# Moving the splits of three segment weights and the loads of an x chunk in a gated attention mix, and giving two value tiles other PSUM banks

## The chip, the cores and the metric

The kernel runs on one core of a Trainium2 chip. The metric is the device time of one execution in microseconds; the median of the runs is compared.

## What is computed

A gate mixes two attention layers over the same input `x` of 2048 rows by 512, with 32 heads of 16:

```python
q, k, v = (x @ wqkv) ...                      # A: full softmax attention
p = _softmax(q @ k.T * Dh ** -0.5)
a = (p @ v) @ wo
...
for s in range(4):                            # B: segments of 512 rows
    a_dot = softmax(qs @ ks.T * scale + mask) @ vs
    a_mem = (phi(qs) @ M) / (phi(qs) @ z + 1e-6)
    outs.append(g * a_mem + (1.0 - g) * a_dot)
    M = M + phi(ks).T @ vs;  z = z + phi(ks).sum(over rows)
b = outs @ wo_B
...
g = _sigmoid((x * gate_w).sum(-1))
out = g * a + (1 - g) * b
```

All is float32. `phi(t)` is `t + 1` where t is positive and `exp(t)` elsewhere. B has its own weights `b_wq`, `b_wk`, `b_wv`.

## The kernel before, in words

**Halves.** Each fp32 operand of a projection is split into a high half (a cast to fp32r on ACT, `copy`) and a low half (the difference, on DVE or POOL, `tensor_sub`). A product is three matmuls (line 360: low-high, high-low, high-high). The names end in `h` and `l`: `wvh` and `wvl` are the halves of a `v` weight, `xbh` and `xbl` those of a tile of tag `xb`.

**Slots.** The projections come first, ahead of the attention loop. PE's program is cut into slots of twelve matmuls of 128x128 by 128x512 (`slot`, line 362; all of them bear line 366), each slot into four places (0 to 3) of three matmuls. What other engines do is hung on a slot and a place: `post_at(n, place, f)` names the slot by number, `post(slots, place, f)` counts from the current one. This sets only the order of the instructions in each engine's program; when an instruction runs is decided by its waits. The slots that matter here:

| slots | what PE computes |
|---|---|
| 0 to 7 | A's `v` of x chunks 0 and 1 (a chunk is 512 rows) |
| 8 to 15 | A's `q` tiles of chunks 0 and 1 |
| 16 to 22 | pair tiles of chunks 0 and 1: `k` and the rest of `q` |
| 23 to 26 | v2: A's `v` of the third chunk, one slot for each 128 rows |
| 27 to 30 | v3: A's `v` of the fourth chunk |
| 31 to 37 | pair tiles of chunks 2 and 3: fourteen products m0 to m13, two in a slot |
| 38 to 41 | B's `q` of chunk 0 |
| 42 to 45 | B's `v` of chunk 0 |
| 46 to 49 | B's `k` of chunk 0 |
| 50 on | B's chunk 1, then 2 and 3, in the same order, with the memory's products and the first score maxima between |

**Banks.** PSUM is handed out by three pools: `pr` (two banks, "query products"), `me` (two) and `sm` (four). A pool hands out its buffers in the order in which they were released; a tile that gets a buffer waits until the readers of its former tile are done. ACT reads a `v` product (line 537, `vs<-pair` or `vs<-pr`) and a `q` or `k` product (line 432, `full`); the pair products are read by ACT (line 492, `p`) and DVE (lines 476, 500, 502: `full` and `u`). v3 has its banks from `me`, `me`, `pr`, `pr`; m2 and m3 follow it in the two `me` banks, in slot 32.

**The tile `vs`.** The four copies of a chunk's `v` fill one tile `vs`, which SP stores to DRAM (line 532, `vdA<-vs`). The tile has one buffer, so the copies of the next chunk wait until that store has landed, and so does a POOL memset of its last column (line 536 for v3).

**Staged loads.** `staged` (line 584) takes a weight or x chunk of 512x512 in two halves of two 128x512 loads each, at two given slots and places, into tiles of tag `raw` (three buffers for a half each) or `small` (tag `ph`, four buffers of 128x512), and splits its four pieces at four given slots and places (line 575 the cast on ACT, line 576 the difference). The B weights are loaded by POOL's queue (line 569). `halves` (line 380) does the same for the x chunks of B, with loads by SP's queue at slot `load_slot` and splits from `split_slot` on (lines 402 and 403); `betas` (line 751) is hung on slot 30 and begins with ACT's activation of `gh` at line 752, in front of which stands a table load.

**Other users of the engines there.** ACT makes the casts of the pair tiles' results (line 479) and of `q` and `k` (line 433), SP stores them, DVE and POOL make their low halves (line 485, line 440).

Of the kernel before, what the change touches and what calls it, by code (L numbers as in the profile page):

```python
# [24 lines left out]
KT = D // 128  # L25
# [22 lines left out]
def gated_mix(ctx, tc, x, xT, wqkv, a_wo, b_wq, b_wk, b_wv, b_wo, beta, gate_w, out):  # L48
    nc = tc.nc
# [283 lines left out]
    with ExitStack() as p0:  # L333
        wp = p0.enter_context(tc.tile_pool(name="wp", bufs=1))
        raws = p0.enter_context(tc.tile_pool(name="raws", bufs=3))
        xp = p0.enter_context(tc.tile_pool(name="xp", bufs=1))
        vp = p0.enter_context(tc.tile_pool(name="vp", bufs=1))
        wk = p0.enter_context(tc.tile_pool(name="wk", bufs=2))
# [15 lines left out]
        now = [0]  # L354
        posted = {}

        def post(slots, place, f):
            posted.setdefault((now[0] + slots, place), []).append(f)
# [17 lines left out]
        def post_at(n, place, f):  # L376
            posted.setdefault((n, place), []).append(f)


        def halves(pool, tag, src, load_slot, split_slot, tiles=None, queue=nc.sync, eng=nc.vector):  # L380

            hold = {}

            def load(i):
                t = tiles[i] and tiles[i]() if tiles else None
                if t is None:
                    t = raws.tile([128, 2, D], F32, tag="raw", name="raw")
                if isinstance(t, list):
                    for k in range(2):
                        queue.dma_start(t[k], src[256 * i + 128 * k:256 * i + 128 * k + 128])  # L390
                        hold["raw", 2 * i + k] = t[k]
                else:
                    queue.dma_start(t, src[256 * i:256 * i + 256].rearrange("(k p) d -> p k d", p=128))
                    for k in range(2):
                        hold["raw", 2 * i + k] = t[:, k]

            def split(k):
                if k == 0:
                    hold[0] = pool.tile([128, KT, D], F32R, tag=tag + "h", name=tag + "h")
                    hold[1] = pool.tile([128, KT, D], F32R, tag=tag + "l", name=tag + "l")  # L400
                w = hold["raw", k]
                nc.scalar.copy(hold[0][:, k], w)
                eng.tensor_sub(hold[1][:, k], w, hold[0][:, k].bitcast(F32))
            if load_slot is None:
                load(0)
                load(1)
            else:
                ls = load_slot if isinstance(load_slot, tuple) else (load_slot,) * 2
                post_at(ls[0], 2, lambda: load(0))
                post_at(ls[1], 3, lambda: load(1))  # L410
            for k in range(KT):
                post_at(split_slot + k // 2, 2 * (k % 2), lambda k=k: split(k))
            return hold

        def xchunk(c):
            return xT[:, c * CH:(c + 1) * CH]
# [107 lines left out]
        def v_tiles(side, w, xs, c, inner=True, behind_=0, banks_=None):  # L524
            vs = vp.tile([128, NG, 4, 4, 17], F32, tag="vs", name="vs")
            if not behind_:
                nc.gpsimd.memset(vs[:, :, :, :, 16:17], 1.0)

            def store():
                flat = vs.rearrange("p g b h e -> p g (b h e)")  # L530
                dst = vdA[:, :, c].rearrange("g p b e -> p g (b e)") if side == "A" else vdB[c].rearrange("p g b e -> p g (b e)")
                nc.sync.dma_start(dst, flat)

            def to_vs(b, ps):
                if b == 0 and behind_:
                    nc.gpsimd.memset(vs[:, :, :, :, 16:17], 1.0)
                nc.scalar.copy(vs[:, :, b, :, 0:16], ps.rearrange("p (g h e) -> p g h e", g=NG, h=4))
            banks = banks_ or [lambda: pr_ps.tile([128, D], F32, tag="pr", name="pr")] * 4
            if not inner:
                pss = [f() for f in banks]  # L540
                for k in range(KT):
                    slot([(pss[b], xs(p, k)[:, b * 128:(b + 1) * 128], w[q][:, k, :], k == 0 and n == 0, k == KT - 1 and n == 2)
                          for n, (q, p) in enumerate(((0, 0), (1, 0), (0, 1))) for b in range(4)])
                for b in range(4):
                    post(behind_, b // 2, lambda b=b: to_vs(b, pss[b]))
                post(behind_, 1, store)
                return vs
            for b in range(4):
                ps = banks[b]()
                whole(ps, lambda a, k: xs(a, k)[:, b * 128:(b + 1) * 128], lambda a, k: w[a][:, k, :])  # L550
                post(behind_, 0, lambda b=b, ps=ps: to_vs(b, ps))
                if b == 3:
                    post(behind_, 0, store)
            return vs
# [29 lines left out]
        def staged(t, src, raws_, splits, queue=nc.sync, keep=None, eng=nc.vector):  # L584

            kept = [] if keep is None else keep
            dest = []

            def load(i):
                kept.extend(raws_[i][0]())  # L590
                load_raw(src[256 * i:256 * i + 256], kept[2 * i:2 * i + 2], queue)

            def split(k):
                if not dest:
                    dest.extend(t())
                split_to(dest[0](k), dest[1](k), kept[k], eng)
            for i in range(2):
                post_at(raws_[i][1], raws_[i][2], lambda i=i: load(i))
            for k in range(KT):
                post_at(*splits[k], lambda k=k: split(k))  # L600
# [4 lines left out]
        def spread(n, place=0):  # L605
            return [(n + k // 2, place + 2 * (k % 2)) for k in range(KT)]
# [6 lines left out]
        xraw = {0: raw_tile(), 1: raw_tile()}  # L613
# [8 lines left out]
        wAv, wAq, wAk = weights("wv"), weights("wq"), weights("wk")  # L622
        xs = {0: in_pool("xa"), 1: in_pool("xb")}
# [27 lines left out]
        def s_split(i, x0, x1, eng=nc.vector):  # L651
            for k in range(2):
                src = (x1[2 + k], x0[k], x1[k], x0[2 + k])[i]
                split_to(ss[i][0][:, k], ss[i][1][:, k], src, eng)
# [65 lines left out]
        def tiles_w(key, tag):  # L720
            def f():
                xs["w"][key] = in_pool(tag) if tag == "xb" else weights(tag)
                return in_tile(xs["w"][key])
            return f
# [1 line left out]
        staged(tiles_x2, xchunk(2), ((raw_tile, 10, 0), (raw_tile, 10, 2)), spread(14), keep=xraw[2])  # L726
        staged(tiles_x3, xchunk(3), ((raw_tile, 11, 0), (small, 11, 2)), spread(17), keep=xraw[3], eng=P)
        staged(tiles_x0, xchunk(0), ((small, 15, 0), (small, 24, 2)), ((23, 1), (23, 3), (27, 1), (27, 3)))
        staged(tiles_w("q", "xb"), b_wq, ((raw_tile, 28, 0), (raw_tile, 28, 2)), spread(31, 1), nc.gpsimd)
        staged(tiles_w("v", "wv"), b_wv, ((raw_tile, 29, 0), (small, 29, 2)), spread(35, 1), nc.gpsimd)  # L730
        staged(tiles_w("k", "wk"), b_wk, ((raw_tile, 34, 0), (raw_tile, 34, 2)), spread(38, 1), nc.gpsimd)
        for k in range(2):
            post_at(18, 3, lambda k=k: s_sums(xraw[2], xraw[3], ((k, P),)))
        for n, i in enumerate((0, 2, 1, 3)):
            post_at((23, 24, 25, 26)[n], 3, lambda i=i: s_split(i, xraw[2], xraw[3]))
        gw = {}
        gmask = wk1.tile([128, NO, 2, DH], F32, name="gmask")
        for h in range(8):
# [33 lines left out]
        sm_bank = lambda: me_sm.tile([128, CH], F32, tag="sm", name="pair")  # L772
        pr_bank = lambda: pr_ps.tile([128, D], F32, tag="pr", name="pr")
# [5 lines left out]
                qk_tile(wAq, xs[c], o, qd["A", o, c], side="A")  # L779
        dk = {(o, c): kd["A", o, c] for o in range(NO) for c in range(NCH)}  # L780
        pair_tiles(wAk, tks, [flat(xs[0]), flat(xs[1])], ss, (0, 1), dk, V)
        v_tiles("A", wAv, lambda a, k: xs[2](a, k), 2, banks_=[sm_bank] * 4)
        v_tiles("A", wAv, lambda a, k: xs[3](a, k), 3, behind_=1, banks_=[me_bank, me_bank, pr_bank, pr_bank])
        pair_tiles(wAk, tks, [lambda a, k: xs[2](a, k), lambda a, k: xs[3](a, k)], ss, (2, 3), dk, P)

# [104 lines left out]
        for c in range(NCH):  # L890
            if c + 1 == NCH:
                load_gate(c)
                post(8, 2, gates)
            for o in range(NO):
                qk_tile(xs['w']['q'], xc, o, qd["B", o, c], pqs.append if c else None, bank=sm_bank if c == 0 and o > 1 else None)
            if c + 1 < NCH:
                xn = halves(*((xp, "xa") if c % 2 else (wp, "wq")), xchunk(c + 1), now[0], now[0] + (4 if c == 0 else 3))
            if c + 1 < NCH:
                post(2, 3, lambda c=c: load_gate(c))
            vs = v_tiles("B", xs["w"]["v"], flat(xc), c)  # L900
            for o in range(NO):
                then = (lambda pk, o=o, c=c, vs=vs: beside_max(lambda: mem_k(o, c, pk, vs))) if c + 1 < NCH else None
                qk_tile(xs['w']['k'], xc, o, kd["B", o, c], then)
            xc = xn
# [421 lines left out]
    n = 0  # L1326
# [81 lines left out]
```

## Time and profile before

| what | us |
|---|---|
| median of 3 runs (1750.44 to 1752.34) | 1751.22 |
| the profiled execution, its own time | 1751.74 |
| span of its trace | 1750.0 |
| PE busy | 1739.6 (99%) |
| DVE busy | 1597.9 (91%) |
| ACT busy | 1436.2 (82%) |
| POOL busy | 736.8 (42%) |
| mean granted TensorE clock | 1.000 of full speed |

The span is counted from the first instruction to the last; the execution's own time is 1.74 us longer. PE's busy time is summed from matmuls that overlap in the pipeline. All times of single instructions in the following are from the start of this span. A row of a timeline has the start, the duration, the engine, the line, the operation, the tiles (written from read) and the shapes; xN are N neighbours of one kind taken together, and brackets hold the idle time of the engine ahead of the row with what ended it.

### The profile page before, as it was taken

The page shows a single profiled execution, that of the slowest core. Times are in us where ns is not written, and L with a number is a line of the kernel's source. Part 1 is how long each engine was busy: PE and PEld are TensorE (multiplying, and loading weights), DVE is VectorE, ACT ScalarE, POOL GpSimd, SP SyncE. Part 2 cuts the span into 40 slices and gives each one's busy share as a digit, 9 for nine tenths or more (in the row PEclk, how much of TensorE's full clock was granted, in tenths as well). Part 3 has the DMA queues.
Part 4 walks back from the last instruction along what each step waited for, and adds up shares of the span by engine and source line. Part 5 has one row for each costly group of instructions (what it writes and reads, how often), then busy time and mean ns, then how long its engine had stood idle before and what let it go on. Part 6 is the DMA issues. An engine that isn't in the chain of part 4 may idle for free.

```text
span 1750.0 us, 41552 instructions
## 1 busy us (share of the span) xinstructions
PE 1739.6 (99%) x15205; PEld 886.2 (51%) x15205; DVE 1597.9 (91%) x3327; ACT 1436.2 (82%) x2763; POOL 736.8 (42%) x992
## 2 busy tenths in 40 slices
PE   9999999999999999999999999999999999999999
PEld 7877775444444444444444444444444444444445
DVE  7756778999999999999999999999999999999931
ACT  6544556888888888888898888888889889888884
POOL 3533232324262418353435353444344353535452
PEclk9999999999999999999999999999999999999999
DMA  6777667334453446454545454444444444544541
GB/s 210 246 241 249 214 214 215 112 107 138 116 157 96 136 135 191 130 143 124 149 127 143 130 143 136 133 136 130 148 125 150 119 132 126 152 115 146 147 156 63
DMA packets 149371, 261.62 MB, mean 149 GB/s; under 512 B 39048, under 2 KB 61608, under 8 KB 148656
## 3 DMA queue, kind: packets, MB, share of 16 engines
q1 hardware_dynamic: 146624, 254.42, 48.7%
q0 software_dynamic: 2400, 4.29, 0.9%
q8 instruction: 121, 1.98, 0.5%
q14 instruction: 82, 0.67, 0.1%
q10 hardware_dynamic: 144, 0.26, 0.1%
HBM read 174.39 MB, written 83.25 MB: 147 GB/s over the span
## 4 chain that ended last, share of the span: by engine, by line
PE 91%; DMA 1%; issue 1%; ACT 0%; POOL 0%; SPq 0%; ACTq 0%; POOLq 0%
PE ops L155 40%; PE st L1044 28%; PE sm L242 14%; PE pr L366 6%; PE sm L155 2%; DMA raw<-xT 0%; PE tps L830 0%; PE mt_ps L232 0%; PE sm L1044 0%; DMA gw<-gate_w 0%; DMA kdA<-q 0%; PE mps L844 0%; DMA kA<-kdA 0%; PE num L803 0%; PE den L807 0%
## 5 line engine op out<-in xcount | busy, mean ns | idle before, releaser
L1067 ACT ACTIVATE p<-st 128x512 f32<-128x512 f32 x2261 | 1191.5, 601 | 147.1 <-PE sm L242 93.8
L275 DVE TENSOR_REDUCE pm<-sm 128x1 f32<-128x512 f32 x2048 | 1276.4, 683 | 9.8 <-PE sm L242 8.7
L242 PE MATMUL sm<-kA,qA 48*128 48x512 f32 x2048 | 661.3, 424 | 0.0
L1044 PE MATMUL st<-qA,kA 50*128 50x512 f32 x2014 | 656.7, 432 | 0.0
L155 PE MATMUL ops<-p,vA 128*17 128x256 f32 (+3 forms) x6360 | 553.1, 445 | 0.2 <-DMA kA<-kdA 0.2
L1044 PEld LDWEIGHTS st<-qA,kA 50*128 50x128 f32 x2014 | 327.0, 185 | 423.2 <-ACT p L1067 380.7
L242 PEld LDWEIGHTS sm<-kA,qA 48*128 48x128 f32 x2048 | 337.5, 185 | 11.0 <-DVE ph L449 3.9
L1168 POOL TENSOR_TENSOR rcp<-rec,minus 128x32 f32<-128x32 f32 x43 | 234.8, 5460 | 77.2 <-DMA rec<-dend 72.5
L290 DVE CUSTOM_DVE_ANT_0 rest<-sm,mask 128x128 f32<-128x128 f32 (+3 forms) x512 | 246.6, 482 | 0.3 <-PE sm L242 0.3
L155 PEld LDWEIGHTS ops<-p,vA 128*17 128x17 f32 x6360 | 129.5, 96 | 215.3 <-issue 183.6
L1048 POOL TENSOR_SCALAR_AFFINE_SELECT p<-p 128x512 f32<-128x512 f32 x128 | 79.5, 637 | 268.7 <-ACT p L1067 264.2
L242 PE MATMUL sm<-kB,qB 48*128 48x128 f32 (+3 forms) x512 | 166.2, 385 | 0.0
L1044 PE MATMUL st<-qB,kB 50*128 50x512 f32 (+1 forms) x495 | 105.4, 329 | 0.3 <-ACT mt L235 0.3
L1044 PEld LDWEIGHTS st<-qB,kB 50*128 50x128 f32 x495 | 68.4, 186 | 62.4 <-ACT p L1067 50.5
L155 PE MATMUL ops<-p,vB 128*17 128x128 f32 (+3 forms) x1504 | 88.3, 350 | 0.0
L214 POOL TENSOR_TENSOR dm<-pm 128x32 f32<-128x32 f32 x32 | 7.9, 247 | 173.2 <-DVE pm L275 173.2
L242 PEld LDWEIGHTS sm<-kB,qB 48*128 48x128 f32 x512 | 79.9, 184 | 0.0
L437 POOL TENSOR_SCALAR mn<-full 128x512 f32<-128x512 f32 x24 | 37.1, 1546 | 76.5 <-ACT full L432 76.5
L223 POOL CAST ms<-pm 128x16 fp32r<-128x16 f32 x32 | 6.3, 196 | 127.6 <-DVE pm L290 127.6
L1184 POOL TENSOR_TENSOR v<-v,inv 128x512 f32<-128x512 f32 x31 | 39.9, 1286 | 26.7 <-DMA inv<-rdA 23.2
L155 PEld LDWEIGHTS ops<-p,vB 128*17 128x17 f32 x1504 | 33.8, 96 | 29.9 <-issue 25.5
L1105 DVE COPY oraw<-ops 128x512 f32<-128x512 f32 x4 | 2.8, 692 | 46.9 <-PE ops L155 36.8
(313 smaller groups left out, 1718.8 us busy)
## 6 DMA issues: line engine op xcount, KB each, us to landing
kA<-kdA SPq DMA_DIRECT2D x256, 128.0 KB
vA<-vdA SPq DMA_DIRECT2D x31, 544.0 KB
kA<-kdA SPq DMA_DIRECT2D x256, 64.0 KB
qB<-qdB SPq DMA_DIRECT2D x192, 64.0 KB
kB<-kdB SPq DMA_DIRECT2D x192, 64.0 KB
kdA<-q SPq DMA_DIRECT2D x32, 256.0 KB
qdB<-q SPq DMA_DIRECT2D x32, 256.0 KB
qA<-qdA SPq DMA_DIRECT2D x64, 128.0 KB
```

What stands on the lines that cost most here:

```text
L155: behind[0] = nc.tensor.matmul(*args, **kw)
L214: nc.gpsimd.tensor_sub(dm, pm[:, :, :, 2:4], pm[:, :, :, 0:2])
L242: nc.tensor.matmul(ps[:, n0:n0 + n], rows(qt[u][:, :, s * 128:(s + 1) * 128], h, 48), rows(k[:, :, k0:k0 + n], h, 48), start=True, stop=True)
L275: nc.vector.tensor_reduce(pm[:, h, s, kc:kc + 1], ps, axis=AX.X, op=ALU.max, negate=True)
L290: nc.vector.tensor_tensor_reduce(out=tri["rest"][:, 0:w], in0=ps[:, n0:n0 + w], in1=tri["mask"][:, CH - w:], scale=-1.0, scalar=3.0e38, op ...
L366: nc.tensor.matmul(ps, l, r, start=start, stop=stop)
L437: nc.gpsimd.tensor_scalar_min(ph["mn"], full, 0.0)
L1044: nc.tensor.matmul(ps[:, n0:n0 + CH - q0], rows(k[:, :, b * 128:(b + 1) * 128], h, 50), rows(q[:, :, q0:], h, 50), start=True, stop=True)
L1048: nc.gpsimd.affine_select(out=x, in_=x, pattern=[[0, 4], [1, 128]], base=0, channel_multiplier=-1, compare_op=ALU.is_ge, fill=0.0)
L1067: nc.scalar.activation(p[:, h], ps, AF.Exp, scale=SCALE)
L1168: eng.tensor_tensor(r, rec, minus, op=ALU.pow)
L1184: eng.tensor_mul(k["v"], k["v"], k["inv"])
```

## The change

It moves work within the part that precedes the attention loop, in four ways. No operation is added or removed, but for the loads of one half of an x chunk, which become two of 128x512.

- `b_wq`: loads from slot 28 to slots 25 and 26, splits from slots 31 and 32 to 29 and 30. `b_wv`: loads from slot 29 to slot 28, splits from slots 35 and 36 to 38 and 39. `b_wk`: loads from slot 34 to slots 32 and 33, splits from slots 38 and 39 to one in each of the slots 41 to 44.
- The splits of the four sums of chunks 2 and 3 stay in slots 23 to 26, in the order 0, 1, 3, 2 in place of 0, 2, 1, 3.
- B's x chunk 1: loads from slot 42 (both halves in `raw` tiles) to slot 34 (first half, in `ph` tiles) and slot 39 (second half, `raw`), splits from slots 46 and 47 to 47 and 48.
- v2's four products have their banks from `pr`, `pr`, `sm`, `sm` in place of `sm` four times.

```diff
-        staged(tiles_w("q", "xb"), b_wq, ((raw_tile, 28, 0), (raw_tile, 28, 2)), spread(31, 1), nc.gpsimd)
-        staged(tiles_w("v", "wv"), b_wv, ((raw_tile, 29, 0), (small, 29, 2)), spread(35, 1), nc.gpsimd)
-        staged(tiles_w("k", "wk"), b_wk, ((raw_tile, 34, 0), (raw_tile, 34, 2)), spread(38, 1), nc.gpsimd)
+        staged(tiles_w("q", "xb"), b_wq, ((raw_tile, 25, 0), (raw_tile, 26, 2)), spread(29, 1), nc.gpsimd)
+        staged(tiles_w("v", "wv"), b_wv, ((raw_tile, 28, 0), (small, 28, 2)), spread(38, 1), nc.gpsimd)
+        staged(tiles_w("k", "wk"), b_wk, ((raw_tile, 32, 0), (raw_tile, 33, 0)), [(41 + k, 3) for k in range(KT)], nc.gpsimd)
...
-        for n, i in enumerate((0, 2, 1, 3)):
-            post_at((23, 24, 25, 26)[n], 3, lambda i=i: s_split(i, xraw[2], xraw[3]))
+        for n, i in enumerate((0, 1, 3, 2)):
+            post_at(23 + n, 3, lambda i=i: s_split(i, xraw[2], xraw[3]))
+        x1 = halves(wp, "wq", xchunk(1), (34, 39), 47, tiles=(small, None))
...
-        v_tiles("A", wAv, lambda a, k: xs[2](a, k), 2, banks_=[sm_bank] * 4)
+        v_tiles("A", wAv, lambda a, k: xs[2](a, k), 2, banks_=[pr_bank, pr_bank, sm_bank, sm_bank])
...
-                xn = halves(*((xp, "xa") if c % 2 else (wp, "wq")), xchunk(c + 1), now[0], now[0] + (4 if c == 0 else 3))
+                xn = halves(*((xp, "xa") if c % 2 else (wp, "wq")), xchunk(c + 1), now[0], now[0] + 3) if c else x1
```

What that does to the order on three engines. First ACT, from the last cast ahead of the store of v2 on (`xah<-ph`), through the copies of v3 (`vs<-pr`) and the casts of `b_wq` (`xbh<-raw`). Before:

```order
73 L575 CAST xah<-ph 128x512 x2
74 L537 COPY vs<-pr 128x8x4x16
75 L752 ACT_TABLE_LOAD
76 L752 ACTIVATE gh<-gh 128x4
77 L537 COPY vs<-pr 128x8x4x16 x2
78 L575 CAST xbh<-raw 128x512
79 L492 COPY p_1074<-pair 128x512
80 L575 CAST xbh<-raw 128x512
```

and of the change:

```order
73 L575 CAST xah<-ph 128x512 x2
74 L537 COPY vs<-pr 128x8x4x16
75 L575 CAST xbh<-raw 128x512 x2
76 L753 ACT_TABLE_LOAD
77 L753 ACTIVATE gh<-gh 128x4
78 L537 COPY vs<-pr 128x8x4x16
79 L575 CAST xbh<-raw 128x512 x2
80 L537 COPY vs<-pr 128x8x4x16
81 L492 COPY p_1080<-pair 128x512
```

The four casts `xbh` now stand in two pairs, one between the first copy of v3 and the table load, one between the second copy and the third.

POOL's program at the loads of the B weights, the memset of `vs` for v3 (line 536), and the low halves of pair results (line 485). Before:

```order
34 L569 DMA raw<-b_wq 128x512 x4
35 L569 DMA raw<-b_wv 128x512 x2
36 L536 MEMSET vs 128x128
37 L569 DMA ph<-b_wv 128x512 x2
38 L569 DMA raw<-b_wk 128x512 x2
39 L485 TENSOR_TENSOR q_1140<-full,q_1139 128x512
40 L569 DMA raw<-b_wk 128x512 x2
```

and of the change:

```order
34 L569 DMA raw<-b_wq 128x512 x4
35 L569 DMA raw<-b_wv 128x512 x2
36 L569 DMA ph<-b_wv 128x512 x2
37 L536 MEMSET vs 128x128
38 L569 DMA raw<-b_wk 128x512 x4
39 L485 TENSOR_TENSOR q_1146<-full,q_1145 128x512
```

The second half of `b_wv` has passed the memset, and the loads of `b_wk` stand together ahead of the first subtraction.

SP's queue, from the last low half of the pair tiles (`kdA`) through B's stores of `q` (`qdB`) to the loads of x chunk 1 (`raw<-xT`), as a piece of the difference; the rows with + are of the change, the last row is of before:

```order
+L482 DMA kdA_88<-q_1253 128x512
+L429 DMA qdB_91<-q_1286 128x512
+L429 DMA qdB_91<-q_1287 128x512
+L393 DMA raw<-xT 128x2x512
+L429 DMA qdB_99<-q_1315 128x512
+L429 DMA qdB_99<-q_1316 128x512
+L429 DMA qdB_107<-q_1338 128x512
+L429 DMA qdB_107<-q_1339 128x512
 L429 DMA qdB_115<-q_1365 128x512
 L429 DMA qdB_115<-q_1366 128x512
-L393 DMA raw<-xT 128x2x512 x2
```

Before, both halves stood behind the eight `qdB` stores; now the second half stands behind two of them, and the first half (`ph<-xT`, line 390) further ahead, among the stores of the pair tiles.

## The prediction

> **What bounds the kernel now.** I read the page first, then PE's waits and timeline in the stretch that the change touches, then the same stretch on ACT, the queues and DVE.
>
> ```profile
> span 1750.0 us, 41552 instructions
> PE 1739.6 (99%) x15205; PEld 886.2 (51%) x15205; DVE 1597.9 (91%) x3327; ACT 1436.2 (82%) x2763; POOL 736.8 (42%) x992
> ```
>
> PE is busy in 99% of the span, so only time in which PE stands still can be won. The order of the attention loop that begins near 286 us isn't changed; what is changed lies in slots 23 to 50. In PE's timeline, each row below but the first, third and fourth is the first matmul after a stop (columns: start, duration, then the instruction; in brackets the idle time and what ended it).
>
> ```profile
> 74.54 0.39 PE L366 MATMUL pair<-wvh,x 128*128 128x512 f32 x1
> 75.53 0.50 PE L366 MATMUL pair<-wvh,x 128*128 128x512 f32 x1 [0.61 <-DVE full L476]
> 75.87 0.40 PE L366 MATMUL pair<-wvl,x 128*128 128x512 f32 x1
> ...
> 95.61 0.61 PE L366 MATMUL pair<-kA,tk 128*128 128x512 f32 x2
> 96.29 0.50 PE L366 MATMUL pair<-kA,kB 128*128 128x512 f32 x1
> ...
> 103.81 0.50 PE L366 MATMUL pair<-x,wkl 128*128 128x512 f32 x1 [0.44 <-DVE u L500]
> ...
> 129.82 0.50 PE L366 MATMUL pr<-wvh,xal 128*128 128x512 f32 x1 [1.21 <-ACT vs L537]
> ...
> 139.84 0.50 PE L366 MATMUL pr<-xah,wkl 128*128 128x512 f32 x1 [1.57 <-ACT vs L537]
> ...
> 146.27 0.50 PE L366 MATMUL pr<-xah,wkl 128*128 128x512 f32 x1 [0.56 <-ACT full L432]
> ```
>
> Two matmuls in a row (x2) take 0.61 us together where one takes 0.39, so they start 0.22 to 0.23 apart; twelve make a slot of 2.72. A stop costs more than its bracket: from 74.54 to 75.53 are 0.99 us where 0.23 was due (0.76), and the step behind it is 0.34 instead of 0.23, so 0.87 for a bracket of 0.61. I add 0.27 to each bracket: slot 25 loses 0.88, slot 35 0.71, slot 44 1.48, slot 47 1.84, slot 49 0.83. The stop at 96.29 has no bracket; the second matmul of the row ahead started at 95.83, 0.23 later was due, so 0.23 (and the restart) are lost. It is the second half of slot 32, the pair product m3, in the second `me` bank, which the third segment of v3 had. These are the terms; the rest asks which go.
>
> **The slot 25 stop goes, and slot 32 takes it.** With the first two v2 products in `pr` banks, slots 25 and 26 get the two `sm` banks whose readers come first, read long before. PE arrives 0.88 earlier at slot 32. There ACT's copies of v3 decide.
>
> ```profile
> 76.68 1.13 ACT L575 CAST xah<-ph 128x512 fp32r<-128x512 f32 x2
> 77.72 1.14 ACT L575 CAST kA<-ph 128x512 fp32r<-128x512 f32 x2
> ...
> 83.79 1.16 ACT L575 CAST xah<-ph 128x512 fp32r<-128x512 f32 x2
> 93.65 0.59 ACT L537 COPY vs<-pr 128x512 f32<-128x512 f32 x1 [8.70 <-DMA vdA<-vs]
> 94.26 1.28 ACT L752 ACT_TABLE_LOAD   x1
> 95.55 0.20 ACT L752 ACTIVATE gh<-gh 128x4 f32<-128x4 f32 x1
> 95.66 1.05 ACT L537 COPY vs<-pr 128x512 f32<-128x512 f32 x2
> ```
>
> ACT stands 8.70 us until the store `vdA<-vs` of the third chunk has landed, because the tile `vs` has one buffer. The copy that frees m3's bank is the first of the two at 95.66; PE restarts at 96.29. The casts ahead of the store are ACT's own backlog from 76.68 to 84.9, which no PE time shortens; the store goes out when they do. So the landing stays where it is however early PE comes. New is that the first two `xbh` casts (slot 29 instead of 31) now stand between the first copy and the table load: two casts take 1.04 (76.68 to 77.72). They can't run in the 8.70 us, since they stand behind the blocked copy. m3 then starts at 96.29 + 1.04 = 97.33 plus whatever the landing moves. Against before, PE is 1.04 **later** there: the gain of slot 25 is gone in the wait, and 1.04 more.
>
> **The landing itself.** The second half of `b_wv` stood behind a POOL memset that waits for the same landing; now it is issued ahead of it.
>
> ```profile
> 83.98 0.38 SPq L532 DMA_DIRECT2D vdA<-vs  x1
> ...
> 84.53 1.07 POOL L569 DMA_DIRECT2D raw<-b_wv  x2
> 93.69 0.32 POOL L536 MEMSET vs<- 128x128 f32 x1 [8.09 <-DMA vdA<-vs]
> 94.15 1.06 POOL L569 DMA_DIRECT2D ph<-b_wv  x2
> ```
>
> So these two loads move from 94.15 to about 85.6. The view of the DMA queues from 80 to 100 us (slices of 0.5 us):
>
> ```profile
> GB/s 246 234 147 176 242 152 111 139 401 352 172 98 84 44 299 369 412 365 411 418 379 431 374 311 224 24 0 0 0 0 66 115 377 369 123 0 0 0 0 0
> q0 software_dynamic: 640, 2.10, 35.3%
> raw<-b_wv POOLq DMA_DIRECT2D x2, 256.0 KB, 6.8
> ph<-b_wv POOLq DMA_DIRECT2D x2, 256.0 KB, 3.0
> ```
>
> From 87 to 92.5 us the engines move 300 to 430 GB/s, and nothing from 93 to 95. The `raw` pair beside the store needs 6.8 us, the `ph` pair alone 3.0. Queue 0 (eight loads) took 35.3% of 20 us, 7.1 us of each engine, so two loads take 1.8. The landing moves by nothing (the two follow the `raw` pair, whose landing lies at 84.53 + 6.8 = 91.3, when most of the store is out) up to 1.8 (the store waits for all of it). Earlier is excluded: nothing is taken from these engines ahead of it. I take 0.9, the middle, since the rows lie as near to one end as to the other. The Trainium skill, "DMA: Bandwidth & Descriptors", section "Queues, rings and completion order", says that each engine takes turns between its queues, packet by packet, draining one packet before it switches. By that rule the store isn't spared, and the sum would go by the upper part of the bounds; the 6.8 against 3.0 agrees in direction.
>
> **The later stops.** They hang on ACT and DVE being late, and on two loads.
>
> ```profile
> 103.08 0.68 DVE L500 TENSOR_TENSOR u<-pair,p 128x512 f32<-128x512 f32 x1
> ...
> 109.34 2.00 DVE L576 TENSOR_TENSOR wvl<-raw,wvh 128x512 fp32r<-128x512 f32 x1 [1.74 <-ACT wvh L575]
> ...
> 119.10 1.28 DVE L476 TENSOR_TENSOR full<-pair,u 128x512 f32<-128x512 f32 x2
> ```
>
> Slot 35 waits for the `u` at 103.08, ahead of which DVE had two `xbl` splits. Now all `xbl` are done before; slot 34 ends its m4 near 103.0 (97.33 + 1.47 + 2.72 + 1.36, and 0.16 to the end of the last matmul), `u` ends at 103.7, and slot 35 is due at 104.2. The stop of 0.71 goes, with 0.5 to spare.
>
> ```profile
> 119.86 1.22 ACT L479 CAST q<-full 128x512 fp32r<-128x512 f32 x2 [1.40 <-DVE full L476]
> 120.99 1.14 ACT L575 CAST wkh<-raw 128x512 fp32r<-128x512 f32 x2
> 122.03 0.58 ACT L432 COPY full<-pr 128x512 f32<-128x512 f32 x1
> ...
> 128.66 0.62 ACT L433 CAST q<-full 128x512 fp32r<-128x512 f32 x1 [1.47 <-DMA qdB<-q]
> 129.19 1.07 ACT L537 COPY vs<-pr 128x512 f32<-128x512 f32 x2
> ...
> 138.68 0.62 ACT L402 CAST wqh<-raw 128x512 fp32r<-128x512 f32 x1 [5.22 <-DMA raw<-xT]
> 139.21 0.58 ACT L537 COPY vs<-pr 128x512 f32<-128x512 f32 x1
> ```
>
> Slot 44 waits for the copy at 129.19. ACT was late there: the bank of slot 38 (start 103.81 + 0.11 + 3 x 2.72 = 112.1, full 2.9 later at 115.0) was read at 122.03, behind DVE's pair chain that ends at 120.38 (the row 119.10) and two `wkh` casts. Four `wvl` splits lay inside that chain (2.00, then three of 0.69, and the waits for their casts). They now follow it. The chain should end with its last product plus 2 us: slot 37 ends near 112.4, so about 114.9. ACT then has slot 38's bank read by about 116, and the `v` copy of slot 42 comes when its product ends, near 126.2 to 126.9, 1.9 ahead of slot 44 (due 128.7). The 1.48 goes.
>
> Slot 47 waits for the copy at 139.21, which stands behind a cast that waits for the next x chunk, `raw<-xT`.
>
> ```profile
> 132.91 1.44 SPq L393 DMA_DIRECT2D raw<-xT  x2
> ```
>
> It needs 5.8 us from issue to the cast (132.91 to 138.68). Its two halves are now issued at slots 34 and 39; SP's queue holds stores of pair tiles ahead of them, so I put them at about 107 and 120: landed 15 us ahead of slot 47. The 1.84 goes. The 0.83 of slot 49 (ACT reading `full` behind the same late casts) goes too, with only 0.4 to spare; if not, it costs at most that 0.83.
>
> What pays for it: the moved splits. Casts and splits of `b_wv` now come behind slot 38, four DVE splits of 0.69, done by about 120.3 against slot 42 at 123.3: cover 3.0. Those of `b_wk`, one a slot from 41 to 44, are done at about 130.8 against slot 46 at 134.2: cover 3.4. A price that can eat the cover:
>
> ```profile
> 107.15 1.29 POOL L485 TENSOR_TENSOR q<-full,q 128x512 fp32r<-128x512 f32 x1 [6.82 <-ACT q L479]
> ```
>
> The `wvl` at 109.34 took 2.00 us, not 0.69, while POOL did its second such subtraction from 109.49. After the change POOL's last two can meet two moved splits: up to 2.6 us, within 3.0. The Trainium skill, "SBUF — State Buffer", section "SBUF: two separate sides", speaks against the new place: DVE and GpSimd hold one port pair by turns, for a whole instruction. The 2.00 against 0.69 agrees.
>
> **The sum**, against the profiled execution: −0.71 −1.48 −1.84 −0.83 = −4.86; +1.04 at slot 32; +0.9 for the landing: **−2.9**. The profiled execution took 1751.74 us (span 1750.0), 0.52 over the median of the runs shown, 1751.22. So 1748.8 for that execution, and 1748.3 as a median. Behind slot 50 PE follows its products in the order of before, and a shift carries to the end.
>
> **Rivals.**
> - *The landing doesn't move.* For it: most of the store is out by 91.3. Against it: 6.8 against 3.0. Then −3.8: 1747.4.
> - *The landing moves by all of 1.8.* Then −2.0: 1749.2.
> - *The steps of the `k` tiles bound instead.* From slot 47 on ACT's exponential may wait for POOL's minimum, since POOL has a row of small loads between those minima; if that holds slots 47 and 49 where they are, 1.84 and 0.83 stay: −0.2, 1751.0. Against it: POOL's minimum follows ACT's copy, which comes earlier.
> - *The moved weight splits come late (slower).* Before, `wkh` of slot 38, place 1, due at 112.8, ran at 120.99: 8.2 late. If that lag stays, the last `wvl` (slot 39, place 3: 117.2 + 8.2 + 1.2 for cast and split = 126.6) misses its product at 125.3 by 1.3, slot 44 keeps its 1.48, and the last `wkl` (slot 44, place 3) misses slot 46 by 8.2 + 1.2 − 5.4 = 4.0. Sum: −0.71 −1.84 −0.83 +1.04 +0.9 +1.3 +4.0 = +3.9: 1755.1. It decides from a lag of 4.2 us at slot 44; against it, the lag came from the `wvl` splits in the pair chain, which are gone.
>
> **How the numbers follow.** Forecast 0.43, landing unmoved 0.30, moved by all 0.12, `k` steps 0.07, late splits 0.08. A measurement of this kernel tells about 0.2% from no change, 3.5 us: under 1747.7 is faster, over 1754.7 slower. The unmoved case is faster, with a fifth of the forecast's cases (landing under 0.3): 0.38. Late splits: slower, 0.08. The rest is the same, 0.54. The range holds the first three cases: 1747.4 to 1749.2, with 0.9 on either side for what the three runs of before differ from their median and for the cover of slot 49: 1746.5 to 1750.1. Left out are the last two, 0.15.
>
> **What would show it.** After: no stop at slot 25; m3 near 97.3 to 99.1 with the wait on `vs`, preceded by two `xbh` casts and the table load; ACT's first v3 copy at 93.65 to 95.5; slot 35, 44 and 47 without a stop. Wrong would be a stop at slot 42 or 46 on `wvl` or `wkl`, a first v3 copy earlier than 93.65, or slot 49 (146.27 before) starting elsewhere than 142.3 to 144.1 (97.33 + 1.47 for the half slot with its restart + 16 x 2.72, and 0 to 1.8 for the landing).

## The result and the profile after

The changed kernel took 1748.88 us (median of 15 runs, 1746.71 to 1751.46) where the kernel before, measured beside it, took 1752.04: a ratio of 0.9984, interval 0.9976 to 0.9992, or about 2.8 us less. A second comparison (the run `after_again` below) gave 1748.05 against 1752.29, ratio 0.9978, interval 0.9968 to 0.9987, about 3.9 us less. The forecast was 1748.3, which is 2.9 less than the median it started from. One run of the kernel before in each of the first two sets (6709 and 4443 us) and one of `banks_alone` below (8124 us) took several times as long as all others, and the ratios leave them out.

The profiled execution is one of two of the 15 whose mean granted clock was 0.998; it took 1751.46. The page of that execution:

```profile
span 1749.7 us, 41555 instructions
PE 1740.2 (99%) x15205; PEld 889.0 (51%) x15205; DVE 1596.5 (91%) x3327; ACT 1436.3 (82%) x2763; POOL 736.6 (42%) x992
```

Its span is only 0.3 us shorter than that of before, though the stops at slots 25, 35, 44, 47 and 49 are gone. These are all the rows of PE with idle time ahead of them between 69 and 150 us, against five before:

```profile
95.72 0.50 PE L366 MATMUL pair<-kA,kB 128*128 128x512 f32 x1 [1.88 <-ACT vs L537]
98.75 0.80 PE L366 MATMUL pair<-kA,kB 128*128 128x512 f32 x1 [1.34 <-ACT vs L537]
```

Both are in slot 32: m2 and m3, each waiting for the copy of v3 that frees its bank. ACT shows why (the same rows as before, with the two `xbh` casts where the order puts them):

```profile
95.08 0.59 ACT L537 COPY vs<-pr 128x512 f32<-128x512 f32 x1 [9.49 <-DMA vdA<-vs]
95.56 1.14 ACT L575 CAST xbh<-raw 128x512 fp32r<-128x512 f32 x2
96.72 1.28 ACT L753 ACT_TABLE_LOAD   x1
98.01 0.21 ACT L753 ACTIVATE gh<-gh 128x4 f32<-128x4 f32 x1
98.13 0.57 ACT L537 COPY vs<-pr 128x512 f32<-128x512 f32 x1
```

The store landed 1.43 later than before (first copy 95.08 against 93.65) and the second copy began 3.05 behind the first instead of 2.01. So m3 starts at 98.75 instead of 96.29, 2.46 later: 1.43 and 1.04. What then ate the rest of the gain is in the table by stages of the same execution. Its columns are the stretch and its length, the busy time of PE with its matmuls, of PEld, DVE, ACT and POOL, then the granted clock, the DMA share and GB/s:

```profile
93.50:98.00 4.50, 2.03 (x8) 1.05 (x6) 1.29 (x2) 2.91 (x4) 0.52 (x2) 0.91 0.09 32
98.00:101.00 3.00, 2.25 (x5) 1.82 (x6) 2.31 (x8) 2.69 (x7) 1.03 (x3) 0.50 0.49 175
101.00:104.00 3.00, 3.00 (x8) 2.31 (x7) 1.12 (x2) 1.10 (x2) 0.90 (x2) 0.50 0.61 181
104.00:107.00 3.00, 3.00 (x15) 2.46 (x14) 2.70 (x5) 0.59 (x1) 0.00 (x0) 1.00 1.05 373
```

Behind the two stops PE ran at half its clock until 104: eight matmuls in 3 us where 15 fit from 104 on. That cost about 2.4 us (m3 to slot 44 takes 33.85 us here and 31.42 in `after_again`), and it is a matter of the execution, as the next section shows.

### The profile page after: what moved, and what is told of

It reads as the page before. It is cut to its first block, busy times and chain, and to the rows that moved or that the text cites. A ratio compares the mean times of both kernels' runs of the same rounds, so it can differ in the third digit from the quotient of the medians.

```text
span 1749.7 us, 41555 instructions
## 1 busy us (share of the span) xinstructions
PE 1740.2 (99%) x15205; PEld 889.0 (51%) x15205; DVE 1596.5 (91%) x3327; ACT 1436.3 (82%) x2763; POOL 736.6 (42%) x992
## 4 chain that ended last, share of the span: by engine, by line
PE 98%; ACT 1%; DMA 1%; DVE 0%; issue 0%; ACTq 0%; SPq 0%
PE ops L155 40%; PE st L1045 28%; PE sm L242 14%; PE pr L366 9%; PE pair L366 4%; PE sm L155 2%; DMA vdA<-vs 1%; PE mt_ps L232 0%; PE tps L831 0%; PE sm L1045 0%; DMA vs<-wqkv 0%; PE mps L845 0%; ACT p L1068 0%; ACT kA L575 0%; PE num L804 0%; PE den L808 0%
## 5 line engine op out<-in xcount | busy, mean ns | idle before, releaser
L440 DVE TENSOR_TENSOR q<-full,q 128x512 fp32r<-128x512 f32 x40 | 29.5, 741 | 18.3 <-ACT q L433 18.2
```

The source lines that it names most:

```text
L440: nc.vector.tensor_sub(q2, full, q1.bitcast(F32))
```

## The experiments

Eleven runs follow; `after_again` and `both_again` repeat a kernel. The starts of slots in the table are those of the profiled executions; "landing" is the start of ACT's first copy of v3, which follows the landing of the store `vdA<-vs`. The columns from m3 on are what the forecast is held against; a profile gives them to a hundredth, while the total time moves by some 2 to 4 us from run to run. But a profile is one execution, and the landing differs between executions (see `wv_behind`). From slot 49 to the end of the span the thirteen profiles take 1603.1 to 1605.6 us, so a shift at slot 49 carries to the end, but for the 2.5 us by which these differ. A median should be compared within its own set only: the kernel before took 1752.29 beside `after_again` to `casts_ahead`, 1752.44 beside `x1_alone` to `both`, and 1751.49 beside `wq_back` to `both_again`.

| kernel | slot 25 | landing | m3 | slot 44 | slot 49 | median, us | ratio to before [95%] |
|---|---|---|---|---|---|---|---|
| before | 75.53 | 93.65 | 96.29 | 129.82 | 146.27 | | |
| changed, clock 0.998 | 74.63 | 95.08 | 98.75 | 132.60 | 146.20 | 1748.88 | 0.9984 [0.9976, 0.9992] |
| after_again | 74.60 | 93.98 | 97.64 | 129.06 | 142.66 | 1748.05 | 0.9978 [0.9968, 0.9987] |
| banks_undone | 76.54 | 94.38 | 98.05 | 129.47 | 143.06 | 1748.89 | 0.9981 [0.9972, 0.9990] |
| wv_behind | 75.08 | 93.19 | 96.86 | 128.28 | 141.88 | 1747.97 | 0.9974 [0.9965, 0.9984] |
| casts_ahead | 74.87 | 94.17 | 96.32 | 127.62 | 141.22 | 1747.76 | 0.9972 [0.9963, 0.9981] |
| x1_alone | 74.72 | 92.11 | 95.13 | 128.53 | 142.29 | 1749.52 | 0.9987 [0.9978, 0.9996] |
| banks_alone | 74.82 | 94.47 | 97.10 | 130.71 | 146.69 | 1752.07 | 1.0000 [0.9991, 1.0009] |
| splits_alone | 75.23 | 94.64 | 98.31 | 129.74 | 143.62 | 1749.44 | 0.9985 [0.9976, 0.9994] |
| both | 74.89 | 92.44 | 95.29 | 126.57 | 140.17 | 1746.46 | 0.9967 [0.9954, 0.9979] |
| wq_back | 74.66 | 95.18 | 97.81 | 129.96 | 143.56 | 1749.34 | 0.9988 [0.9979, 0.9997] |
| both_sm | 76.29 | 92.89 | 96.83 | 128.11 | 141.71 | 1747.29 | 0.9974 [0.9965, 0.9983] |
| both_again | 74.64 | 91.15 | 95.04 | 126.32 | 139.92 | 1746.47 | 0.9973 [0.9962, 0.9984] |

**The changed kernel again (`after_again`).** No edit.

> The changed kernel once more, beside the three below on the same chip. Theory: slot 49 starts about 2.8 us earlier than before (143.5 against 146.27) when the granted clock stays 1.000, and m3 is held by the copy that follows the store, about 98.7. In the profiled execution at clock 0.998 slots 32 and 33 ran at half clock and lost some 2.4 us; if that is a matter of chance, this run's profile shows full clock there and a median about 2.8 us under the kernel before. Rival: the half clock belongs to the order, then every profile of it has it, and the median lies within 0.5 us of before.

The granted clock was 1.000 in the profile and in all 11 runs. PE's stops in the first fence, ACT's two copies in the second:

```profile
span 1746.7 us, 41555 instructions
...
94.62 0.50 PE L366 MATMUL pair<-kA,kB 128*128 128x512 f32 x1 [0.81 <-ACT vs L537]
97.64 0.50 PE L366 MATMUL pair<-kA,kB 128*128 128x512 f32 x1 [1.37 <-ACT vs L537]
```

```profile
93.98 0.59 ACT L537 COPY vs<-pr 128x512 f32<-128x512 f32 x1 [9.41 <-DMA vdA<-vs]
...
97.03 0.57 ACT L537 COPY vs<-pr 128x512 f32<-128x512 f32 x1
```

The order of the waits is the same, 3.05 between the copies too; only the landing is 1.1 earlier, the first stop shorter, and the clock stays whole. Slot 49 starts 3.61 earlier than before (142.66 against 146.27), more than the 2.8 expected, since the landing came at 93.98. Of the 26 runs of this order (15 and 11), two show 0.998: the half clock comes with some executions, not with the order as such.

**The banks undone in the changed kernel (`banks_undone`).**

```diff
-        v_tiles("A", wAv, lambda a, k: xs[2](a, k), 2, banks_=[pr_bank, pr_bank, sm_bank, sm_bank])
+        v_tiles("A", wAv, lambda a, k: xs[2](a, k), 2, banks_=[sm_bank] * 4)
```

> The changed kernel with v2 in four sm banks again. Theory: the stop of 0.88 us at slot 25 comes back and m2 and m3 wait 0.88 less for the same copies, so the time is that of the changed kernel within 0.3 us: about 2.8 us under before. Rival: the stop at slot 25 was worth its 0.88; then about 1.9 us under before.

```profile
76.54 0.50 PE L366 MATMUL pair<-wvh,x 128*128 128x512 f32 x1 [1.42 <-DVE full L476]
...
98.05 0.50 PE L366 MATMUL pair<-kA,kB 128*128 128x512 f32 x1 [0.80 <-ACT vs L537]
```

Slot 25 stops for 1.7 us (a bracket of 1.42 and 0.27), more than in the profile of before. Yet m3 starts as far behind the first copy in both kernels (98.05 - 94.38 = 3.67, 97.64 - 93.98 = 3.66), and slot 49 lies 0.40 later with a landing 0.40 later. By the trace the stop at slot 25 is worth nothing here, as the theory had it; nor does it delay the landing, which hangs on a chain of other engines (see `wv_behind`). The times alone don't settle it: the ratios (0.9981 and 0.9978) don't tell the two kernels apart, but the medians differ by 0.84 us the rival's way.

**The same edit by itself (`banks_alone`)**, the kernel before with `pr`, `pr`, `sm`, `sm`.

> The kernel before with only the banks of v2 changed. Theory: the stop of 0.88 at slot 25 goes and the wait of m3 in slot 32 grows by as much (from 0.23 to about 1.1), so slot 33 and all behind it start where they did, within 0.2 us, and the time is that of before. Rival: the 0.88 is kept, 0.9 under before.

```profile
95.11 0.50 PE L366 MATMUL pair<-kA,kB 128*128 128x512 f32 x1 [1.09 <-ACT vs L537]
97.10 0.50 PE L366 MATMUL pair<-kA,kB 128*128 128x512 f32 x1 [0.34 <-ACT vs L537]
```

The stop at slot 25 is gone, and one of 1.09 stands at slot 32, where before had none in brackets. Ratio 1.0000. Slot 49 starts 0.42 later, with a landing 0.82 later.

**The loads of `b_wv` behind the store again (`wv_behind`).**

```diff
-        staged(tiles_w("v", "wv"), b_wv, ((raw_tile, 28, 0), (small, 28, 2)), spread(38, 1), nc.gpsimd)
+        staged(tiles_w("v", "wv"), b_wv, ((raw_tile, 28, 0), (small, 29, 2)), spread(38, 1), nc.gpsimd)
```

> The changed kernel with the second half of b_wv issued behind the memset that waits for the store, as before. Theory: the store lands 1.4 us earlier (ACT's first copy of v3 at 93.7 instead of 95.1), m3 starts that much earlier, and the time falls by 1.4: about 4.2 us under before. Rival: the store was late for another reason (the b_wq loads or the store itself vary by run); then the copy stays near 95 and the time that of the changed kernel, 2.8 under before.

```profile
93.19 0.59 ACT L537 COPY vs<-pr 128x512 f32<-128x512 f32 x1 [8.33 <-DMA vdA<-vs]
```

The landing is 0.79 earlier than in `after_again`, and slot 49 follows by 0.78 (141.88). One profile each wouldn't prove it, for the store itself is issued at other times (SP's row of it is at 82.95 in `both_again`, at 85.22 in `banks_alone`). These times can be followed back to a point ahead of every edit, near 53 us, where a cast of ACT waits until a store of `q` has landed. The rows of the kernel before, and below them those of `x1_alone`:

```profile
53.36 0.62 ACT L433 CAST q<-full 128x512 fp32r<-128x512 f32 x1 [0.88 <-DMA qdA<-q]
...
74.80 1.27 DVE L476 TENSOR_TENSOR full<-pair,u 128x512 f32<-128x512 f32 x2
...
83.98 0.38 SPq L532 DMA_DIRECT2D vdA<-vs  x1
```

```profile
52.38 0.62 ACT L433 CAST q<-full 128x512 fp32r<-128x512 f32 x1 [0.43 <-DMA qdA<-q]
...
73.82 1.28 DVE L476 TENSOR_TENSOR full<-pair,u 128x512 f32<-128x512 f32 x2
...
82.99 0.38 SPq L532 DMA_DIRECT2D vdA<-vs  x1
```

In the thirteen profiles the cast starts anywhere from 52.33 to 54.63, DVE's row follows it by 21.40 to 21.44 us (21.67 in `wv_behind`), and the store follows that row by 9.17 or 9.18, with either choice of banks. So the length of the store has to be read apart from its issue.

From SP's row to the first copy the kernels with the second half of `b_wv` behind the store have 9.12 to 9.67 us (before, `x1_alone`, `banks_alone`, `wv_behind`; mean 9.34), the six with it beside the store 9.40 to 11.10 (mean 10.53), the three with all of `b_wv` behind it 8.15 to 8.44 (mean 8.26). In the mean, each half beside the store costs its landing about 1.1 to 1.2 us; one profile of the six (`banks_undone`, 9.40) lies within the first group. The earlier loads of `b_wq` aren't the cause, since `wv_behind` has them too.

The views of the DMA queues agree; this is the same stretch, 80 to 100 us, in `after_again`:

```profile
raw<-b_wv POOLq DMA_DIRECT2D x2, 256.0 KB, 6.8
ph<-b_wv POOLq DMA_DIRECT2D x2, 256.0 KB, 7.2
```

Beside the store the second half takes 7.2 us to land, alone it took 3.0.

**The casts and the table load into ACT's wait (`casts_ahead`).**

```diff
-        staged(tiles_w("q", "xb"), b_wq, ((raw_tile, 25, 0), (raw_tile, 26, 2)), spread(29, 1), nc.gpsimd)
+        staged(tiles_w("q", "xb"), b_wq, ((raw_tile, 25, 0), (raw_tile, 26, 2)), spread(28), nc.gpsimd)
...
-        post_at(30, 0, betas)
+        post_at(28, 0, betas)
```

> The changed kernel with the four casts of b_wq at slot 28 and the gate's activation with its table load at slot 28, so that all stand ahead of ACT's first copy of v3, in its wait for the store. Theory: the second copy follows the first at once (landing + 1.2 instead of landing + 3.7); m3 is then held only by m2, which waits for the first copy (start 95.7), so m3 starts at about 97.1 instead of 98.75: 1.65 us less, about 4.4 us under before. Rival: ACT isn't what holds PE there, or the b_wq loads land too late and hold the first copy; then no gain, 2.8 under before or less.

```profile
94.17 0.58 ACT L537 COPY vs<-pr 128x512 f32<-128x512 f32 x1 [5.50 <-PE pair L366]
94.66 0.62 ACT L575 CAST xbh<-raw 128x512 fp32r<-128x512 f32 x1
95.17 1.08 ACT L537 COPY vs<-pr 128x512 f32<-128x512 f32 x2
```

(The first copy's bracket names PE, which had written that bank long before; it is the store that ends the wait.) The second copy now follows the first by 1.00 instead of 3.05 (one cast of the four still lies between). m3 starts at 96.32, 2.15 behind the first copy instead of 3.66, and slot 49 1.44 earlier than in `after_again`. In the median only 0.3 of that shows (1747.76 against 1748.05): intervals of this width don't resolve 1.4 us, and in the profiled execution PE had two stops of 0.59 and 0.43 at 674 and 683 us on loads of the attention loop (`rec<-odB`, `qB<-mt`) and reached the end with no gain over `after_again`.

**The x chunk alone (`x1_alone`)**: the kernel before with the line `x1 = halves(...)` and its use.

> The kernel before with only the loads and splits of B's x chunk 1 moved. Theory: the stops at slots 47 (1.84) and 49 (0.83) go and nothing else changes, so slot 50 starts 2.7 us earlier than before and the time is 2.7 under before; the stops at slots 25, 35 and 44 stay. Rival: ACT's late chain, not the load, holds slots 47 and 49 as well; then less than 1 us.

From slot 44 to slot 49 it takes 13.76 us (128.53 to 142.29), before 16.45 (129.82 to 146.27): 2.69 less, the 1.84 and 0.83 (2.67) within 0.02. Slot 49 itself is 3.98 earlier, because in this execution the landing was early (92.11) and slot 25 had no stop, both for the cast at 52.38 shown above; the program up to slot 34 is that of before. The theory had the stop at slot 25 stay; here it went, but not through this edit. Ratio 0.9987.

**The weights' loads and splits alone (`splits_alone`)**: the kernel before with the three changed `staged` lines.

> The kernel before with only the loads and splits of b_wq, b_wv and b_wk moved. Theory: m3 starts 1.04 later for the two casts and about 0.9 later for the landing, the stops at slots 35 (0.71) and 44 (1.48) go, so slot 46 starts 0.2 to 0.3 earlier than before; the stop at slot 47 for the x load stays or grows, since its raw buffers now come free later: time between 0.3 under and 1.5 over before. Rival, the moved splits come late: stops at slots 42 and 46 on the low halves, about 3.9 over before.

Up to slot 44 as expected: m3 at 98.31 (landing 94.64), then 31.43 to slot 44 where before took 33.53, 2.10 less against 0.71 + 1.48 = 2.19. Slots 42 and 46 have no stop, so the moved splits weren't late. (The new order of the four sum splits was never run alone. The changed kernel has it and takes 31.42 on this stretch, so it is worth nothing there.) But the stop at slot 47 is gone too, and the theory had it stay; of that at slot 49, 0.27 of 0.83 is left. SP's queue and ACT show the reason:

```profile
130.18 1.95 SPq L393 DMA_DIRECT2D raw<-xT  x2
```

```profile
135.82 0.62 ACT L402 CAST wqh<-raw 128x512 fp32r<-128x512 f32 x1 [2.57 <-DMA raw<-xT]
136.34 0.58 ACT L537 COPY vs<-pr 128x512 f32<-128x512 f32 x1
```

The x loads stand in SP's queue behind the stores of B's `q`, and these wait for ACT. With ACT no longer late, they are issued at 130.18 instead of 132.91, the cast waits 2.57 instead of 5.22, and the last copy of `v` runs at 136.34 instead of 139.21, ahead of slot 47 (due about 137.9). So **either** edit takes the stop at slot 47 away: the stretch from slot 44 to 49 is 2.69 shorter with the x loads alone, 2.57 with the weights alone, and 2.85 with both. The ratios (2.3 and 2.6 us alone, 2.8 and 3.9 together) point the same way, but their intervals of about 1.6 us on either side wouldn't show it.

**The splits of `b_wq` back (`wq_back`)**: the changed kernel with `spread(31, 1)` for `b_wq`.

> The changed kernel with the splits of b_wq back at slots 31 and 32. Theory: the two casts no longer stand between the first and the second copy of v3, so the second copy starts 2.0 us behind the first (as before) instead of 3.0, and slot 33 starts 1.04 earlier for the same landing; the four splits are again beside the pair chain, so up to 0.7 comes back as a stop at slot 35: between 0.3 and 1.0 us under the changed kernel at slot 36. Rival: the casts are no cost there, and slot 36 stands where it did.

```profile
95.18 0.59 ACT L537 COPY vs<-pr 128x512 f32<-128x512 f32 x1 [9.62 <-DMA vdA<-vs]
...
97.19 1.06 ACT L537 COPY vs<-pr 128x512 f32<-128x512 f32 x2
```

```profile
105.34 0.50 PE L366 MATMUL pair<-x,wkl 128*128 128x512 f32 x1 [0.44 <-DVE u L500]
```

The second copy comes 2.01 behind the first, 1.04 less than in the changed kernel, and slot 33 starts 4.12 behind the landing (99.30) instead of 5.16 (99.14 in `after_again`), as worked out; the stop at slot 35 is back with the bracket it had before. Counted from the landing, slot 36 starts 13.02 behind it (108.20), in `after_again` 13.32 (107.30): 0.3 gained, the lower end of what was expected. The landing of this execution is 1.2 later, so its slot 49 shows none of it; nor does the median (1749.34, ratio 0.9988), for which the other landings aren't known.

**Both causes of slot 32 taken away (`both`, `both_again`, `both_sm`)**: `casts_ahead` with all of `b_wv` behind the memset, the third with v2 in `sm` banks.

```diff
-        staged(tiles_w("v", "wv"), b_wv, ((raw_tile, 28, 0), (small, 28, 2)), spread(38, 1), nc.gpsimd)
+        staged(tiles_w("v", "wv"), b_wv, ((raw_tile, 29, 1), (small, 29, 2)), spread(38, 1), nc.gpsimd)
```

> The changed kernel with the casts of b_wq and the table load ahead of ACT's first copy of v3, and with both halves of b_wv issued behind the memset that waits for the store. Theory: the store has the DMA engines nearly alone and lands at about 92 instead of 94 to 95, neither m2 nor m3 waits, no stop is left from slot 23 to 49, and slot 49 starts about 5.9 us earlier than before (0.88 + 0.34 + 4.86, less 0.2): about 5.5 under before. Rival: the store's length is its own, it lands at 93.2 as with half of b_wv behind, m2 waits some 0.3, and 5.3 are gained at slot 49; or the loads of b_wv and b_wk, now all behind the landing, come late for slots 42 and 46.

> The same with pr, pr, sm, sm, once more beside it: about 5.6 us under the kernel before, slot 49 near 140.2, no stop from slot 23 to 49.

> The kernel with the casts and the table load ahead of the copy and all of b_wv behind the store, with v2 in four sm banks again. Theory: now that nothing waits at slot 32, the stop at slot 25 is paid in full: slot 49 starts later by that stop (0.3 to 1.4 in the profiles so far, 0.9 in the middle) than with the pr banks, and the time is about 0.9 over it. Rival: the copy of v3 still holds slot 32, and the banks make no difference here either.

The whole stretch of `both` as one row of the table by stages, and below it that of before:

```profile
69.00:150.00 81.00, 81.00 (x362) 66.44 (x361) 50.93 (x83) 43.85 (x78) 37.64 (x50) 1.00 0.78 261
```

```profile
69.00:150.00 81.00, 76.56 (x333) 61.20 (x332) 47.27 (x73) 40.18 (x72) 33.81 (x47) 1.00 0.71 234
```

PE is busy without a gap. The store lands at 92.44 and 91.15, nothing waits at slot 32, and slot 49 starts at 140.17 and 139.92, 6.1 and 6.35 earlier than before. The medians, 1746.46 and 1746.47, are the lowest of all, by the ratios (0.9967 and 0.9973) 5.8 and 4.7 us under before; `casts_ahead` has 0.9972, and both intervals overlap those of the changed kernel. With `sm` banks the stop at slot 25 is now paid:

```profile
76.29 0.50 PE L366 MATMUL pair<-wvh,x 128*128 128x512 f32 x1 [1.25 <-DVE full L476]
```

1.52 us there, and slot 49 1.79 later than in `both_again` (0.23 of it was there at slot 23 already), the median 0.8 over it (1747.29 against 1746.47). The same edit that by the trace is worth nothing ahead of a wait is worth its stop when that wait is gone.

## Why the prediction was right, point by point

| step | forecast, us | `after_again` against before, us |
|---|---|---|
| stop of slot 25, lost again at slot 32 | 0 | 0 (`banks_undone`, `banks_alone`) |
| two casts ahead of the second copy | +1.04 | +1.04 (3.05 - 2.01) |
| the landing | +0.9, 0 to 1.8 | +0.33 (0.39 earlier issue, 0.72 longer); in the mean of the kernels 1.2 longer |
| stops of slots 35 and 44 | -2.19 | -2.11 (31.42 from m3 to slot 44 for 33.53, and m3 at 97.64) |
| stops of slots 47 and 49 | -2.67 | -2.85 (13.60 from slot 44 to 49 for 16.45) |
| sum at slot 49 | -2.9 | -3.61 (the rows add up to -3.59) |

The steps hold one by one, and the sum at slot 49 (142.66) lies in the 142.3 to 144.1 that the prediction named. In the first profile it does not: slot 49 starts at 146.20 there, because of 2.4 us at half clock, for which the prediction has no term. In time, too, the difference is what counts, since the forecast 1748.3 starts from a median of three runs, 1751.22, and the later sets of before lie at 1751.49 to 1752.44: -2.9 was forecast, and the ratios give -2.8 (-4.2 to -1.4) and -3.9 (-5.6 to -2.3). These hold the rival with an unmoved landing, -3.8, as well, and the first also the other, -2.0.

The uncertain term was the landing, and it stayed so: in the six profiles with the early loads it moved by 0.3 to 1.5 against the one profile of before. Two things make it up. The store takes 1.2 us longer in the mean, within the bounds of 0 to 1.8; that the forecast took 0.9, the middle, was a guess. And the store isn't issued at a fixed time, though the prediction took it so; its issue moves between 82.95 and 85.22, behind a chain that starts near 53 us. It holds that an earlier PE doesn't move it.

Four things were seen wrongly or not at all, without harm to the sum at slot 49. PE waits twice in slot 32, not once: m2 waits for the first copy (bracket 0.81), which m3's wait covers. The stop at slot 47 was put down to the place of the x loads alone; `splits_alone` shows that without ACT's lateness they come early enough from their old place, so the one stop had two cures. Some readings are off: the casts `xah` at 83.79 run behind the last copy of the third chunk (83.32), for which the store waits, and not ahead of the store (the same goes for ACT's order under "The change"); the pair chain's end is 112.4 + 2 = 114.4 where 114.9 stands; 130.8 for the last `b_wk` split leaves out its cast and itself (it ended at 131.1 in `after_again`, 3.4 ahead of slot 46). And the moved `b_wv` splits ended later than the forecast 120.3:

```profile
111.88 0.69 DVE L485 TENSOR_TENSOR q<-full,q 128x512 fp32r<-128x512 f32 x1 [3.82 <-DMA kdA<-q]
...
115.96 1.28 DVE L476 TENSOR_TENSOR full<-pair,u 128x512 f32<-128x512 f32 x2
118.49 2.47 DVE L576 TENSOR_TENSOR wvl<-raw,wvh 128x512 fp32r<-128x512 f32 x2 [1.25 <-ACT wvh L575]
...
122.09 0.68 DVE L576 TENSOR_TENSOR wvl<-ph,wvh 128x512 fp32r<-128x512 f32 x1
```

```profile
118.82 1.60 POOL L485 TENSOR_TENSOR q<-full,q 128x512 fp32r<-128x512 f32 x1
```

DVE stood 3.82 us until the store of a pair tile had landed, so the pair chain ended at 117.24 instead of 114.9, and the casts of `b_wv` came behind it. Then the first two splits took 2.47 beside POOL's subtraction instead of 1.3, and the last ended at 122.8. Slot 42 began at 123.6 and needs it 2.0 later. No stop came of it, with 2.8 us left, since the need lies in the slot's last quarter; against the start of slot 42, as the prediction counted its cover of 3.0, 0.8 was left. The price beside POOL was foreseen in kind; the 1.2 us that it took here were hidden.

Of the rivals, the late splits and the `k` steps didn't come. The two on the landing can't be told from the forecast: they lie 0.9 to either side of it, and in the four profiles with half of `b_wv` behind the store the landing alone moves from 92.11 to 94.47.

## What to carry to other kernels

Ask of a stop that you mean to remove what holds the engine next: with a store to land at slot 32, by the traces an edit of 0.9 to 1.7 us was worth nothing, and with that wait gone it was worth all of its stop (1.5 us). Work that stood in ACT's order behind a copy waiting for the store was paid when the copy was released (1.04 us for two casts); most of it put ahead of the copy, three casts and the table load, fitted in the wait, and m3 came 1.5 us sooner after the landing. Where two edits cure one stop, their gains don't add.

## What the runs showed of the hardware

- **Half clock after two short stops.** In the profiled execution of the changed kernel PE had six matmuls between 93.8 and 98.75, with brackets of 1.88 and 1.34 around them, and its granted clock was 0.50 from before 98 to 104 (0.91 in the mean of the 4.5 us to 98: half clock from about 97.2, so 6.8 us). Two of that kernel's 15 runs had the mean clock 0.998 and took 1751.4 us, the 13 others 1746.7 to 1749.6 at 1.000. In `after_again`, brackets of 0.81 and 1.37 left the clock whole, in `wq_back` those of 1.96 and 0.33. The Trainium skill, "TensorE: Matmul & The Clock Gate", section "Part 1: The HAM clock gate", tells of a free-running window of about 3.4 us in which the activity of PE decides between full and half clock. The 6.8 us agree with two such windows, and the dependence on the execution with a window that doesn't start with the kernel. PE was not idle for a whole such window: of the 3.4 us ahead of 97.2 it was busy for 1.5. Runs of the kernel before show 0.999 or 0.998 too (16 of 32 in one set, 5 of 27 and 2 of 23 in others); in which stage wasn't seen, since its profile is at 1.000.
- **The stop at slot 25 is not a fixed size.** It was 0.88 in the profile of before, 1.7 in `banks_undone`, 1.5 in `both_sm`, 0.55 in `splits_alone` and none in `x1_alone`. In the four with a stop, slot 25 starts 0.73 or 0.74 behind DVE's `full` row (74.80 in before), which follows the cast near 53 us; so both this stop and the issue of `vdA<-vs` move with the landing of one store of `q` there, by up to 2.3 us between profiles. What moves that landing stays open.
